# One weight transfer issued as 119 + 9 partitions at the end of a weight stream

## The chip, the cores and the metric

The kernel runs on one core of one Trainium2 chip. A core has five engines that work beside each other and are tied by semaphores: TensorE (PE, matrix products; its weight loads are shown as PEld), VectorE (DVE), ScalarE (ACT), GpSimd (POOL) and SyncE (SP). Sixteen DMA engines move data between the memory outside the core (DRAM) and the 128 partitions of the core's memory; POOL, SP and ACT issue transfers to them, each through a queue of its own. A transfer signals that it has landed through a semaphore, which the engines raise by one each, sixteen in all. The metric is the time of one execution in microseconds (us), as the device measures it; lower is better.

## The reference

The reference runs a sliding-window attention and feeds its result, 8 batches of 576 positions with 512 channels, to a spectral mixing layer:

```python
X = np.fft.rfft(x, axis=1)                       # x: 8 x 576 x 512, out of the attention
Xr, Xi = (np.real(X[:, :n_modes]), np.imag(X[:, :n_modes]))      # 64 modes
Yr = np.einsum('bmd,mde->bme', Xr, w_r) - np.einsum('bmd,mde->bme', Xi, w_i)
Yi = np.einsum('bmd,mde->bme', Xr, w_i) + np.einsum('bmd,mde->bme', Xi, w_r)
Y[:, :n_modes] = Yr + 1j * Yi
y = np.fft.irfft(Y, n=S, axis=1)
u = x + y
return (u + np.maximum(u @ w_ch, 0.0)).astype(np.float32)
```

Each of the 64 modes has a real and an imaginary weight matrix of 512 x 512 float32. Together `w_r` and `w_i` are 128 MB, and each number of them is used once for each batch. They have to come in from DRAM once.

## The kernel before, in words

The kernel does four things that overlap. It computes the attention (units of four score blocks, lines 252 to 345) and the forward transform of its result into `XQ`, with tables of sines. It streams the mode weights in and multiplies them with the transformed input (`mode_half`, line 176). It computes `x @ w_ch` tile by tile (line 610) while the stream goes on. At last it transforms the mixed modes back, adds, applies the rectifier and stores 36 tiles of 128 x 512 (lines 786 to 926).

The weights come in groups of four modes. `steps` (line 98 on) lists (group, half of the 512 input channels); for each step there is one transfer of `w_r` and one of `w_i`. The last steps are those of groups 12 and 13 (`LAST` and `LAST + 1`), so the last transfer brings the `w_i` half of group 13, modes 52 to 55. A transfer turns float32 in DRAM into bfloat16 on its way. Its tile is 128 partitions x 4 modes x 1024 numbers, 1 MB as it lands and 2 MB as it is read: each partition and mode is one row of 2 KB. The page's sizes are those of the landed data.

The list `wlist` (lines 103 to 114) holds these transfers; each entry has a list `parts` of the pieces that it is issued in. For nearly all entries `parts` has one piece of four modes. One early entry (`ONES`) is spread over three separate entries. For the last entry of all, `parts` has three pieces, `[(p, p + 1), (p + 2,), (p + 3,)]`: two modes (512 KB landed, 1 MB read), one mode, one mode.

`load_weights` (line 142) issues transfers from POOL in the order of `wlist`, as far as a buffer is free: a ring `ringA` of three tiles and, earlier, `ringB` of five and some memory lent by other tiles. A transfer into a ring tile waits until TensorE has done the matmuls that read the tile's old contents. At the end of the stream only `ringA` is in use, so POOL issues a transfer when TensorE has finished the one three before it.

`mode_half` issues one step's matmuls for `w_r` or `w_i`. For the last one (`ending`, line 180) the matmuls are sorted by mode, so that those of modes 52 and 53 wait for the first piece alone, those of 54 for the second and those of 55 for the third. The order of TensorE's instructions is the order in which this code calls them. Just ahead of the last half TensorE is given the left-over `x @ w_ch` jobs and the first output tile's start (`late["first"]`, `tail_xw(0)`). Behind it comes the tail: the halves of the last product are cast on VectorE and ScalarE (`cast_halves`, line 626), turned on TensorE (line 648 on), multiplied by `w_ch` (lines 1006 and 1014), and then each output tile takes part in a chain of matmuls, adds and a store.

Of the kernel before, what the change touches and what calls it, by code (L numbers as in the profile page):

```python
# [16 lines left out]

NRA = 3
NRB = 5
WARM = 8  # L20
NEG = -1.0e30
MAGIC = 12582912.0
# [4 lines left out]
def kernel(  # L27
# [10 lines left out]
    nc = tc.nc  # L38
# [10 lines left out]
    HALF = DM // 2  # L49
    NJ = 2  # L50
# [5 lines left out]
    def pool(name, bufs=1, **kw):  # L56
        opened.append(tc.alloc_tile_pool(name=name, bufs=bufs, **kw))
        return opened[-1]
# [32 lines left out]
    ringA = pool("ringA", bufs=NRA, side="right", reuse_waits="tile")  # L91
    ringB = pool("ringB", bufs=NRB, side="right", reuse_waits="tile")
    EARLY = 10
# [11 lines left out]
    for at, (grp, hb) in enumerate(steps):  # L105
        for ri in range(2):
            p = 4 * grp
            if (at, ri) == ONES:
                parts = [[(p, p + 1)], [(p + 2,)], [(p + 3,)]]
            elif (at, ri) == (len(steps) - 1, 1):  # L110
                parts = [[(p, p + 1), (p + 2,), (p + 3,)]]
            else:
                parts = [[(p, p + 1, p + 2, p + 3)]]
# [20 lines left out]
    held = {"a": [], "b": [], "y": []}  # L134
    room = {"a": NRA, "b": NRB, "y": NLY}
    nload = 0
# [5 lines left out]
    def load_weights(n):  # L142
        nonlocal nload
        while nload < len(wlist):
            at, parts, hb, ri = wlist[nload]
            if 2 * n <= sum(len(ps) for ps in parts):
                return
            if nload in lent:
                w = lent[nload]
            else:  # L150
                open_to = "a" if at >= 2 * EARLY else "aby" if at < EARLY + 2 else "ab"
                h = min(open_to, key=lambda h: held[h][0] if len(held[h]) == room[h] else -1)
                if len(held[h]) == room[h]:
                    if held[h][0] not in spent:
                        return
                    held[h].pop(0)
                held[h].append(nload)
                if h == "y":
                    w = lentY
                else:  # L160
                    w = {"a": ringA, "b": ringB}[h].tile([128, 4, NJ, DM], BF16, name="wi" if ri else "wr", tag="wt")
            src = moe_w_i if ri else moe_w_r
            to = 0
            for ps in parts:
                nc.gpsimd.dma_start(  # L165
                    out=w[:, to:to + len(ps)],
                    in_=src[ps[0]:ps[-1] + 1, HALF * hb:HALF * hb + HALF, :].rearrange("g (p j) e -> p g j e", j=NJ))
                for i, p in enumerate(ps):
                    wtiles[p, hb, ri] = w[:, to + i]
                to += len(ps)  # L170
            nload += 1
            n -= to
# [24 lines left out]
    with tc.manual_schedule():  # L197
# [165 lines left out]
        warm = ps_m.tile([128, DM], FP32, name="warm", tag="misc")  # L363
        for _ in range(WARM):
            nc.tensor.matmul(out=warm, lhsT=idle[:, 0:128], rhs=idle, start=True, stop=True)
# [16 lines left out]
        for nm in ("k", "q", "v"):  # L382
            load(1, nm)
        LEAD = 4
        load_weights(LEAD)
        nc.gpsimd.iota(Kb, pattern=[[64, NBLK]], base=0, channel_multiplier=0,
                       allow_small_or_imprecise_dtypes=True)
# [77 lines left out]
        def early_step(it):  # L465
            nonlocal step
            grp = step
            psm = ps_m.tile([128, DM], FP32, name="psm", tag="misc")
            for ri in range(2):
                mode_half(psm, grp, 0, ri, True, True)  # L470
                load_weights(due(it) - loaded())
            nc.scalar.copy(out=Yacc[grp], in_=psm)
            step += 1
# [4 lines left out]
        for it in range(-3, NU + 3):  # L478
# [23 lines left out]
            g = starts.get(it + 2)  # L502
# [3 lines left out]
            g = starts.get(it + 1)  # L506
            if g is not None and g + 2 < NG:
                load(g + 2, "v")
            if it >= 0:
                for f in trig[0:2]:  # L510
                    f()
                del trig[0:2]
            load_weights(due(it) - loaded())
        do_dft(NG - 1)
        while step < EARLY:
# [255 lines left out]
        ps, pu = {}, {}  # L771
# [292 lines left out]
```

## Time and profile before

| what | us |
|---|---|
| median of three runs | 435.42 |
| lowest and highest of them | 435.29, 435.87 |
| the profiled execution: its own time | 435.06 |
| the profiled execution: its span | 433.3 |
| TensorE busy in it | 333.3 (77%) |
| VectorE, ScalarE, POOL busy | 230.1, 180.0, 101.5 |
| share of DMA in the chain that ended last | 60% |
| mean granted TensorE clock | 0.881 |

The span runs from the first to the last instruction of the program; the execution's time has 1.8 us around it. Names on the left of an arrow are written, names on the right are read: `wi<-in_moe_w_i_dram` is a transfer of `w_i` from DRAM into a ring tile named `wi`. `psm` is the accumulator that `mode_half` writes, `XQ` and `XL` hold the transformed input, and L188 is the line of its matmul. In the chain of work that ended last, each piece is what released the next one; a DMA piece is counted from its issue to its landing, so a transfer that was issued early shows the time that it stood in the queue too. The DMA view of a stretch of time gives the mean busy share of the 16 engines in tenths and the GB/s that they moved, in 40 equal slices.

### The profile page before, as it was taken

To read this page: it belongs to the slowest core of one execution; us is meant where nothing else is said; L and a number is where in the kernel's file an instruction comes from. 1 tells how busy PE (TensorE), PEld (TensorE's weight loads), DVE (VectorE), ACT (ScalarE), POOL (GpSimd) and SP (SyncE) were. 2 spreads that over 40 slices of the span, in tenths; PEclk is the share of its full clock that TensorE was granted. 3 is DMA by queue.
4 is the path that set the end of the run, shared out by engine and by line. 5 is a ranking of instruction groups with operands and counts; after the bars stand their busy time and mean duration, and the time that the engine had idled before them with its cause. 6 is when DMAs were issued, how large, how long until landed. Compare 5 with 4: busy or idle time off the path is not lost.

```text
span 433.3 us, 11049 instructions
## 1 busy us (share of the span) xinstructions
PE 333.3 (77%) x4802; PEld 216.2 (50%) x4802; DVE 230.1 (53%) x472; ACT 180.0 (42%) x322; POOL 101.5 (23%) x150
## 2 busy tenths in 40 slices
PE   6999999998999998974208354666676779779994
PEld 3666767576767676651104122334343445445652
DVE  8588687876676776855104111302131315662894
ACT  5666667575766665520202100122121213334742
POOL 8422223222231231113102100012111112110990
PEclk9999999999999999976558656759888869999998
DMA  8999999999999999999999999999999999994798
GB/s 211 211 211 212 211 212 211 211 211 212 211 212 211 211 212 211 212 213 211 212 259 213 217 212 212 212 212 211 209 212 213 208 211 212 212 212 79 248 357 294
DMA packets 47280, 93.64 MB, mean 216 GB/s; under 512 B 2688, under 2 KB 3136, under 8 KB 47232
## 3 DMA queue, kind: packets, MB, share of 16 engines
q0 software_dynamic: 41008, 81.73, 99.7%
q1 hardware_dynamic: 5328, 9.77, 6.6%
q10 hardware_dynamic: 896, 1.44, 0.9%
q8 instruction: 37, 0.61, 0.5%
q14 instruction: 11, 0.09, 0.1%
HBM read 163.58 MB, written 9.44 MB: 399 GB/s over the span
## 4 chain that ended last, share of the span: by engine, by line
DMA 60%; PE 25%; issue 7%; DVE 3%; ACT 2%; POOL 1%; SPq 0%; DVEq 0%; POOLq 0%
DMA wr<-in_moe_w_r_dram 37%; DMA wi<-in_moe_w_i_dram 16%; DMA rawk<-in_k_dram 7%; PE tr L231 4%; PE psm L188 3%; PE s L278 2%; PE s L290 2%; PE s L270 2%; PE pt L298 2%; PE vb L243 2%; PE o L318 1%; PE psz L786 1%; PE psz L610 1%; DMA out_dram<-ut 1%; PE pst L786 1%
## 5 line engine op out<-in xcount | busy, mean ns | idle before, releaser
L610 PE MATMUL psz<-wch,tr 128*128 128x512 f32 x176 | 63.7, 496 | 11.3 <-DMA wch<-in_moe_w_ch_dram 11.0
L756 DVE CAST xw<-psz 128x512 fp32r<-128x512 f32 x36 | 24.9, 692 | 89.0 <-PE psz L610 89.0
L282 DVE TENSOR_REDUCE mx<-s 128x4 fp32r<-128x512 f32 x72 | 49.6, 689 | 26.7 <-PE s L278 26.4
L584 ACT CAST tr<-ptx 128x512 fp32r<-128x512 bf16 x36 | 21.1, 587 | 101.2 <-PE ptx L603 101.2
L188 PEld LDWEIGHTS <-XQ 128*32 128x32 bf16 x448 | 18.6, 176 | 76.0 <-issue 51.7
L165 POOL DMA_DIRECT2D wi<-in_moe_w_i_dram x32 | 23.4, 732 | 101.4 <-PE psm L188 68.2
L188 PE MATMUL psm<-wi,XQ 128*32 128x512 bf16 x208 | 20.8, 475 | 33.9 <-DMA wi<-in_moe_w_i_dram 33.9
L610 PEld LDWEIGHTS psz<-wch,tr 128*128 128x128 f32 x176 | 37.5, 236 | 18.4 <-issue 11.6
L292 ACT ACTIVATE p<-s 128x512 bf16<-128x512 f32 x72 | 39.7, 603 | 12.8 <-PE s L290 12.8
L165 POOL DMA_DIRECT2D wr<-in_moe_w_r_dram x27 | 20.4, 757 | 98.7 <-PE psm L188 50.6
L188 PE MATMUL psm<-wr,XQ 128*32 128x512 bf16 x184 | 19.3, 501 | 27.4 <-DMA wr<-in_moe_w_r_dram 26.8
L235 ACT COPY kT<-tr 128x576 bf16<-128x576 bf16 x32 | 23.2, 725 | 21.3 <-PE tr L231 21.3
L270 PE MATMUL s<-mask_t,ident_bf 128*128 128x512 bf16 x72 | 28.4, 395 | 0.9 <-ACT p L292 0.8
L278 PE MATMUL s<-kT,qT 64*64 64x128 bf16 (+1 forms) x576 | 29.0, 220 | 0.0
L301 DVE COPY pts<-pt 128x1024 bf16<-128x1024 bf16 (+1 forms) x40 | 25.2, 630 | 5.3 <-PE pt L298 4.0
L235 ACT COPY qT<-tr 128x576 bf16<-128x576 bf16 x32 | 23.3, 729 | 10.3 <-PE tr L231 10.3
L278 PEld LDWEIGHTS <-qT 64*64 64x64 bf16 x576 | 17.7, 106 | 18.0 <-issue 17.5
L290 PE MATMUL s<-mx,ident_r 128*128 128x512 f32 x72 | 26.2, 437 | 0.0
L235 ACT COPY vT<-tr 128x576 bf16<-128x576 bf16 x32 | 23.3, 728 | 4.0 <-PE tr L231 3.8
L298 PE MATMUL pt<-ident_bf,p 128*128 128x128 bf16 x288 | 23.3, 220 | 1.5 <-issue 1.3
L635 DVE TENSOR_TENSOR stg<-psm,Yfour 128x512 bf16<-128x512 f32 x10 | 6.9, 691 | 32.8 <-PE psm L188 32.8
L218 POOL DMA_DIRECT2D rawk<-in_k_dram x15 | 8.1, 541 | 63.8 <-PE tr L231 57.6
(211 smaller groups left out, 611.3 us busy)
## 6 DMA issues: line engine op xcount, KB each, us to landing
wi<-in_moe_w_i_dram POOLq DMA_DIRECT2D x29, 1024.0 KB, 19.1
wr<-in_moe_w_r_dram POOLq DMA_DIRECT2D x27, 1024.0 KB, 18.1
out_dram<-ut SPq DMA_DIRECT2D x28, 256.0 KB, 2.8
rawv<-in_v_dram POOLq DMA_DIRECT2D x16, 288.0 KB, 15.4
rawk<-in_k_dram POOLq DMA_DIRECT2D x15, 288.0 KB, 14.4
rawq<-in_q_dram POOLq DMA_DIRECT2D x15, 288.0 KB, 14.3
x_sb<-in_moe_w_r_dram POOLq DMA_DIRECT2D x2, 1024.0 KB, 15.7
Yfour<-in_moe_w_i_dram POOLq DMA_DIRECT2D x1, 1024.0 KB, 14.5
```

Source lines behind the costliest of these rows:

```text
L165: nc.gpsimd.dma_start(out=w[:, to:to + len(ps)], in_=src[ps[0]:ps[-1] + 1, HALF * hb:HALF * hb + HALF, :].rearrange("g (p j) e -> p g j e" ...
L188: nc.tensor.matmul(out=ps[32 * g:32 * g + 32, 0:e], lhsT=of.rearrange("k s b m -> k (s b) m")[:, (3 * j + 1 - ri) * B:(3 * j + 5 - ri) * B ...
L235: nc.scalar.copy(out=to, in_=pt.rearrange("p j n -> p n j"))
L270: nc.tensor.matmul(out=s, lhsT=ident_bf, rhs=mask_t[:, mk], start=True, stop=True)
L278: nc.tensor.matmul(out=s[ro, t, lo:128], lhsT=lq, rhs=kT[ro, 64 * n - 64 + lo:64 * n + 64], start=False, stop=True, skip_group_check=True)
L282: nc.vector.tensor_reduce(out=mx, in_=s, axis=AX.X, op=ALU.max, negate=True)
L290: nc.tensor.matmul(out=s, lhsT=ident_r, rhs=mx.unsqueeze(2).to_broadcast([128, 4, 128]), start=False, stop=True, skip_group_check=True)
L292: nc.scalar.activation(out=p[:, 4 * c2:4 * c2 + 4, :], in_=s, func=ACT_F.Exp, scale=EX_SCALE)
L298: nc.tensor.transpose(out=pt[:, t, :], in_=st[u]["p"][:, t, :], identity=ident_bf)
L301: nc.vector.tensor_copy(out=ps[:, 0:nt, :], in_=pt[:, 0:nt, :])
L610: nc.tensor.matmul(out=pz, lhsT=tr[:, c, :], rhs=wch[:, c, :], start=(c == 0), stop=(c == NDCH - 1))
L756: nc.vector.tensor_copy(out=XW[i], in_=multiply(tr))
```

## The change

The piece of two modes in the last entry is issued as two transfers instead of one: the first takes partitions 0 to 118, the second partitions 119 to 127, both of the same two modes. The two single-mode pieces behind it, and all other transfers, are issued as before. A loop picks the one or two ranges of partitions: two when an entry has several pieces and the piece has two modes, which holds only for that one piece. POOL issues one transfer more; the order on the other engines stays. The matmuls of modes 52 and 53 depend on both transfers.

```diff
+UNEVEN = 119
...
             for ps in parts:
-                nc.gpsimd.dma_start(
-                    out=w[:, to:to + len(ps)],
-                    in_=src[ps[0]:ps[-1] + 1, HALF * hb:HALF * hb + HALF, :].rearrange("g (p j) e -> p g j e", j=NJ))
+                of = src[ps[0]:ps[-1] + 1, HALF * hb:HALF * hb + HALF, :].rearrange("g (p j) e -> p g j e", j=NJ)
+                for lo, hi in ((0, UNEVEN), (UNEVEN, 128)) if len(parts) > 1 and len(ps) == 2 else ((0, 128),):
+                    nc.gpsimd.dma_start(out=w[lo:hi, to:to + len(ps)], in_=of[lo:hi])
                 for i, p in enumerate(ps):
                     wtiles[p, hb, ri] = w[:, to + i]
                 to += len(ps)
```

The rows in DRAM that the two transfers read are the same as before: a mode's 256 channels are dealt to the partitions in pairs, so partition `p` takes channels `2p` and `2p + 1`, 4 KB in a row in DRAM for each mode.

## The prediction

> **What bounds the kernel now.** I read the page's overview first, then the chain of work that ended last, then the DMA view of the seven microseconds in which the weight stream ends, then the order of instructions there.
>
> ```profile
> span 433.3 us, 11049 instructions
> ...
> DMA  8999999999999999999999999999999999994798
> ...
> q0 software_dynamic: 41008, 81.73, 99.7%
> ...
> q8 instruction: 37, 0.61, 0.5%
> ```
>
> The mean busy share of the 16 DMA engines stays at nine tenths in nearly every slice until 396 us, and the queue of POOL's transfers, q0, makes up all of it. The row q8 is fetched program code: 0.5% of 16 x 433.3 us is 35 us, over 37 fetches 0.94 us each, on the same engines.
>
> ```profile
> 367.45 13.88 DMA wr<-in_moe_w_r_dram
> 381.33 0.04 issue
> 381.37 0.67 PE psm L188 x16
> 382.04 0.24 PE psp L648 x4
> 382.28 0.08 issue
> 382.36 1.26 POOL wi L165 x2
> 383.62 12.62 DMA wi<-in_moe_w_i_dram
> 396.24 0.04 issue
> 396.28 0.50 PE psm L188 x3
> ```
>
> The chain (start, duration, what) is one weight transfer after another; the last lands at 396.24 us, and TensorE starts on it 0.04 us later. From there the chain runs to the end through TensorE, VectorE and the stores. So the end moves one for one with the landing of the last weight bytes, as long as TensorE has nothing else left to do.
>
> ```profile
> DMA  9999999888785566655555566433223320000000
> GB/s 234 211 187 211 187 211 199 164 152 164 140 152 105 105 117 117 117 94 105 105 94 94 105 117 117 82 70 70 47 47 59 59 35 12 0 0 0 0 0 0
> ```
>
> This is 390 to 397 us in 40 slices of 0.175 us. The stream does not stop at once: 211 GB/s until 391.2, about 105 (half of the engines) from 392.2 to 394.4, about 60 (four engines) until 396.0. The same is in the trace's record of the last transfer's semaphore, which each of the 16 engines raises once: 391.28, .35, .66, .72, 392.18, .42, .58, .86 (eight early engines), 394.59, 395.00, .19, .29, 396.06, .12, .18, .24 (eight late ones). The record gives no engine's number. All 16 keep one pace: full transfers land every 4.95 us on each of them. The lateness is old: the spread was 1.6 us for the transfer that landed at 25.5 us and 5.0 us for that of 198.9, and it grew by about 0.95 us on one engine after another, which is a code fetch's length. [...]
>
> ```profile
> 391.00:393.00 2.00, 2.00 (x12) 1.37 (x9) 0.43 (x1) 1.97 (x4) 0.00 (x0) 1.00 0.74 139
> 393.00:395.00 2.00, 2.00 (x29) 1.26 (x28) 0.00 (x0) 0.59 (x1) 0.00 (x0) 1.00 0.51 95
> 395.00:396.30 1.30, 0.68 (x10) 0.37 (x5) 0.00 (x0) 0.00 (x0) 0.00 (x0) 1.00 0.16 30
> ...
> 394.56 1.10 PE L188 MATMUL psm<-wi,XL 128*32 128x256 bf16 x12
> 396.28 0.60 PE L188 MATMUL psm<-wi,XL 128*32 128x256 bf16 x4 [0.62 <-DMA wi<-in_moe_w_i_dram]
> ```
>
> Last columns: DMA share and GB/s. From 391.0 on, 2.00 x 139 + 2.00 x 95 + 1.30 x 30 = 507 KB land; at 211 GB/s that is 2.40 us, so level engines would finish at 393.4 instead of 396.24. TensorE bounds it tighter: it only reaches the last half's matmuls at 394.56, and 16 of them take 0.67 us (the row at 381.37), so they would end at 395.2 at best, not at 396.88: no dealing of the bytes can gain more than 1.65 us.
>
> **The change part by part.** *One more issue on POOL.* The three issues at 382.36 take 0.70, 0.57 and 0.55 us, so a fourth adds 0.55 to 0.70 us before the last one. The last issue would end at about 384.8; the earliest engine comes to that transfer's rows after the one before it, which it finishes at 390.06. Cover is over 5 us on POOL's queue, no other transfer of POOL's follows, and no weight transfer queues behind: cost nothing. If the queue ran dry, it would cost those 0.7 us. SP's and ACT's queues issue nothing between 382 and 398.
>
> *One more wait on TensorE.* The first eight matmuls wait for two semaphores instead of one. The "issue" rows after waits are 0.04 us; it falls at 394.56 at the earliest, before the last landing: nothing, at most 0.04.
>
> *How the bytes are dealt out.* This decides. Two modes are 2 x 128 rows of 2 KB, 16 for each engine. An engine's row costs 4.95 us / 32 = 0.155 us (and 2 KB at 211/16 GB/s = 0.155). All partitions in this trace come in 128s, in 16 equal shares; no row shows 119. If shares must stay equal, 119 = 7 x 17 leaves seven engines with 34 rows each, and nine partitions go to nine engines with 2 rows each. So seven engines gain 18 rows, 18 x 0.155 = 2.79 us, and nine lose 14, 2.17 us (if the nine are the others). If shares may be unequal, at most 8 and 1 partitions meet on one engine, 18 rows instead of 16: +0.31 us; the engine left out is up to 16 rows, 2.48 us, earlier.
>
> [...] No run here shows which holds for 119.
>
> *What it does to the end.* With seven shares, if one of the seven is among the four engines that end at 396.06 to 396.24, the end is there plus 2.79: 398.85 to 399.03, later by 2.61 to 2.79 us. If they touch only the late four of 394.59 to 395.29, it ends at 397.38 to 398.08, later by 1.14 to 1.84. If all seven are early engines, the slowest ends at 392.86 or 392.58 plus 2.79, 395.65 or 395.37, and the late ones at 396.24 - 2.17 = 394.07: earlier by 0.59 or 0.87 us. With sixteen shares: between -0.06 (the engine of 396.24 is the one left out, the next is at 396.18) and +0.31. The unknown so lies between -0.87 and +2.79. I take equal shares, because every transfer of the trace has them, and the seven touching the last four, because seven picked as a run of neighbours (my assumption; a random seven would do worse) miss eight late ones only if the early eight are neighbours too and the run starts on their first or second: 2 of 16 starts, or about one of two if the run always begins at one end of a half. Sum: 0 (POOL) + 0 (TensorE) + 2.7 us. The chain behind it has no cover, so all of it shows: the profiled execution took 435.06 us with its span of 433.3, so 437.76; it lies 0.36 us below the median of 435.42, against which I forecast 438.1.
>
> **The rivals.** *Seven early engines take the extra rows (faster).* The mechanism is a levelling: 34 rows fit into the 3.4 to 5 us by which the early half leads, and the nine light engines get 2.17 us back. For it: the split moves 2.79 us one way and 2.17 us the other, across a gap of 3.4 us between the groups' middles. Against it: it needs the right seven. It decides at the point where no engine ending after 393.45 (396.24 - 2.79) is among the seven. Price -0.59 to -0.87: 434.55 to 434.83. [...]
>
> *Shares over all sixteen (no change).* For it: all 16 engines raise every semaphore here. Against it: no unequal share is seen. -0.06 to +0.31: 435.36 to 435.73.
>
> *Only the less late four are hit.* +1.14 to +1.84: 436.56 to 437.26.
>
> *Something else*, such as slower rows on a crowded engine (a row costs 0.155 us at any time here, also when four engines are left: 8 rows between the increments at 395.02 and 396.24) or an empty queue.
>
> **How the numbers follow.** Seven shares with one of the last four: 0.44, time 438.1, own range 437.9 to 438.4. Less late four: 0.05. Early seven: 0.32. Sixteen shares: 0.13. Something else: 0.06 (0.04 slower, 0.02 faster). The bound of 0.2%, 0.87 us, is about what a measurement of this kernel can tell from no change. The early seven end just at it: half, 0.17, is counted as faster and 0.15 as the same. Faster 0.17 + 0.02 = 0.19; same 0.15 + 0.13 = 0.28; slower 0.44 + 0.05 + 0.04 = 0.53. The range reaches from the early seven to the forecast, with 0.1 to 0.2 us for the scatter of runs (435.29 to 435.87): 434.4 to 438.4.
>
> **What would show it.** In the changed kernel's semaphore record of the 119-partition transfer, seven of the sixteen increments should stand about 2.8 us later, and nine 2.2 us earlier, than the steps before them. If the forecast holds, the tail in GB/s has a stretch of one to seven engines (13 to 92 GB/s) up to about 399 us, and TensorE's wait before its last four matmuls grows from 0.62 to about 3.3 us. If the early seven took it, the tail falls off steeply at 394 to 395.7 and that wait shrinks or goes. With sixteen shares the staircase stays. POOL's group at L165 should have one instruction more of 0.5 to 0.7 us. Wrong would be the forecast if the run of seven avoids the late engines, if shares are unequal, or if TensorE had other work in the gap.

## The result, and the profile after

The changed kernel took 439.86 us (median; 439.5, 440.21, 441.0 and 438.0), the kernel before in the same session 435.55 (435.29 to 435.87): a ratio of 1.0093, with a 95% interval of 1.008 to 1.0105. The change is slower by some 4.3 us. The forecast was 438.1 with a range up to 438.4, so its sign was right and its size was not: about 1.8 us are missing from its sum, as the net of two errors that go opposite ways.

The changed kernel's profiled execution took 439.5 us with a span of 437.7. First its overview (the same rows as before):

```profile
span 437.7 us, 11007 instructions
...
DMA  8999999999999999999999999999999999991798
...
q0 software_dynamic: 41344, 81.73, 98.8%
```

The stream is as full as before until its last slices; the queue q0 moves the same 81.73 MB in 336 packets more. Next its chain of work that ended last (start, duration, what), around the landing:

```profile
382.69 2.07 POOL wi L168 x3
384.76 12.99 DMA wi<-in_moe_w_i_dram
...
397.79 0.72 PE psm L189 x3
...
400.46 1.15 PE psz L1007 x4
401.62 0.85 PE psm L1007 x4
402.47 1.71 PE psp L1015 x4
```

POOL starts the last of its four issues at 384.76 and ends it at 385.33, where 384.8 was worked out; the first engine is through with that piece's predecessor at 388.75, so this costs nothing. The last bytes land at 397.75 instead of 396.24: 1.51 us later, not 2.7. The last three rows are the surprise. In the chain of before the same three groups of matmuls are shorter:

```profile
398.13 0.67 PE psz L1006 x4
398.80 0.48 PE psm L1006 x4
399.28 0.93 PE psp L1014 x4
```

The time from the last landing to the end of the span grew from 37.04 to 39.97 us. So 1.51 + 2.93 = 4.44 us, which is the whole difference between the two profiled executions (439.5 against 435.06), and two thirds of it lie behind the landing, where the prediction has nothing.

The windows view, cut on steps of 3.41 us on which the granted clock changes, shows what happened there. Columns: the stretch, its length, busy time and count of PE, PEld, DVE, ACT and POOL, the granted TensorE clock, the DMA share, GB/s. First the changed kernel, then the one before.

```profile
394.51:397.92 3.41, 1.83 (x16) 0.90 (x15) 0.00 (x0) 0.00 (x0) 0.00 (x0) 1.00 0.17 31
397.92:401.33 3.41, 2.75 (x13) 1.66 (x14) 1.12 (x2) 1.50 (x4) 0.00 (x0) 0.50 0.00 0
401.33:404.74 3.41, 3.41 (x14) 2.22 (x12) 0.42 (x1) 0.84 (x2) 0.00 (x0) 0.50 0.14 38
404.74:408.16 3.42, 3.42 (x21) 1.56 (x20) 3.41 (x6) 3.32 (x7) 2.55 (x3) 1.00 0.51 104
```

```profile
394.91:398.32 3.41, 2.38 (x22) 1.35 (x18) 0.91 (x2) 1.06 (x4) 0.00 (x0) 1.00 0.07 13
398.32:401.74 3.42, 3.42 (x23) 2.11 (x22) 1.80 (x4) 2.24 (x5) 0.27 (x1) 1.00 0.14 38
```

In the stretch in which it waits for the last bytes TensorE was busy for 2.38 of 3.41 us before (0.70) and for 1.83 now (0.54). In the changed kernel the granted clock is 0.50 for the next two stretches, 6.83 us, just as the tail begins; in the one before it stays at 1.00 until 429.05.

TensorE's order of instructions there (start, duration, engine and line, what, count, and in brackets the idle time before with what ended it):

```profile
395.49 0.67 PE L189 MATMUL psm<-wi,XL 128*32 128x256 bf16 x8 [0.54 <-DMA wi<-in_moe_w_i_dram]
396.54 0.60 PE L189 MATMUL psm<-wi,XL 128*32 128x256 bf16 x4 [0.39 <-DMA wi<-in_moe_w_i_dram]
397.79 0.92 PE L189 MATMUL psm<-wi,XL 128*32 128x256 bf16 x4 [0.65 <-DMA wi<-in_moe_w_i_dram]
```

Three waits, 1.6 us together, stand in place of one of 0.62. By the record of the semaphores the pieces of modes 52 and 53, of 54 and of 55 have landed at 395.44, 396.50 and 397.75 us, where it was 393.79, 395.02 and 396.24 before: each comes about 1.5 us later, the first of them too. Last the DMA view of 390 to 401 us in 40 slices of 0.275 us:

```profile
DMA  9999989898978773233222111000000000000000
GB/s 165 179 179 150 143 164 186 164 171 164 179 134 149 142 134 67 45 60 60 52 45 37 30 22 30 15 7 0 0 0 0 0 0 0 0 0 0 0 0 0
```

The busy share holds at 0.7 or more until 394.1; then it falls in a step to 0.2 to 0.3 and about 50 GB/s, four engines of sixteen, and trails off. There is no such step before. The record of the semaphores tells the shares. The sixteen increments of the transfer before the split, and of the 119 partitions:

```
last full transfer  386.76 .91 .97 387.11 .14 .15 388.47 .51 | 389.60 390.26 .34 .39 391.15 .45 .58 .89
119 partitions      387.19 .35 .40 390.63 .65 391.34 .64 392.09 .22 .24 .35 .50 393.79 .98 394.85 395.23
```

Of the early eight, three raise it at 387.19 to 387.40, 0.2 to 0.5 us after the last full transfer: they have no row of it. Five come about 5.3 us after it (388.47 to 393.79 for one), 34 rows of 0.155 us. Two of the late eight have 34 rows as well (389.60 to 394.85). So seven engines got the 119 partitions and nine did not. With sixteen equal shares this execution would have ended at 391.89 + 32 x 0.1547 = 396.84 us (the last engine's end of the last full transfer, and its 32 rows of 2 KB at 4.95 us / 32 each); it ended at 397.75. This end is an estimate. The dealing cost 0.91 us of the 1.51; the other 0.60 is the stream of this execution, which was later before the split.

In the rest of the text "late by" is this difference: the last landing less the equal-share end of the same execution. In the kernel before it is 0.03 us.

### The profile page after: what moved, and what is told of

It is laid out like the page before. It is cut to its first block, busy times and chain, and to the rows that moved or that the text cites. A ratio compares the mean times of both kernels' runs of the same rounds, so it can differ in the third digit from the quotient of the medians.

```text
span 437.7 us, 11007 instructions
## 1 busy us (share of the span) xinstructions
PE 324.7 (74%) x4758; PEld 216.9 (50%) x4802; DVE 229.8 (52%) x472; ACT 180.1 (41%) x322; POOL 102.2 (23%) x151
## 3 DMA queue, kind: packets, MB, share of 16 engines
q0 software_dynamic: 41344, 81.73, 98.8%
## 4 chain that ended last, share of the span: by engine, by line
DMA 52%; PE 34%; issue 6%; ACT 3%; DVE 2%; POOL 1%; DVEq 0%; POOLq 0%
DMA wi<-in_moe_w_i_dram 31%; DMA wr<-in_moe_w_r_dram 21%; PE tr L232 5%; PE s L279 4%; PE s L291 3%; PE pt L299 3%; PE vb L244 3%; PE psm L189 3%; PE o L319 2%; PE s L271 2%; PE psz L787 1%; PE pst L787 1%; PE pst L869 1%; PE px L342 1%; ACT qT L236 1%
## 5 line engine op out<-in xcount | busy, mean ns | idle before, releaser
L611 PE MATMUL psz<-wch,tr 128*128 128x512 f32 x176 | 60.9, 477 | 11.2 <-DMA wch<-in_moe_w_ch_dram 11.0
L611 PEld LDWEIGHTS psz<-wch,tr 128*128 128x128 f32 x176 | 36.3, 229 | 18.0 <-issue 11.6
L331 DVE TENSOR_TENSOR x_sb<-o,r 128x512 bf16<-128x512 f32 x32 | 22.1, 691 | 1.1
```

Of the source, the lines that this page charges most:

```text
L331: nc.vector.tensor_tensor(out=xo.rearrange("p c (h d) -> p c h d", d=64), in0=ov[:, :, :, 0:64], in1=rb, op=ALU.mult)
L611: nc.tensor.matmul(out=pz, lhsT=tr[:, c, :], rhs=wch[:, c, :], start=(c == 0), stop=(c == NDCH - 1))
```

## The experiments

Two questions were open. Where does the landing end up, and why not at +2.7 us? And is the tail's 2.9 us a consequence of TensorE's waits, of the lateness as such, or chance? The theory: the 119 partitions go to seven engines in equal shares, which ones being set by a ring; they make the landing late; TensorE's longer waits let its granted clock fall to one half behind the landing. Rivals: the split costs something in itself; the seven can be moved to early engines, so that the change would be faster; the clock falls for another reason.

Each run was timed beside the kernel before. Times are medians with the lowest and highest; the ratios have 95% intervals.

### The change once more

No edit, a second set of runs.

> The changed kernel once more, to see what of its time repeats. Theory A (unequal dealing plus clock): the sixteen increments of the 119-partition transfer again split into seven that come 34 rows (5.3 us) after those of the transfer before and nine that come within 0.5 us; the granted clock falls to 0.5 for one or two steps of 3.4 us right behind the last weight landing, and the tail from that landing to the end of the span is 39 to 41 us where that happens and 37 us where it does not. Time 438 to 441. Theory B (the tail is longer for another reason, say the stores): the tail is 39 to 41 us at a clock of 1.0 too.

Measured: 440.19 us (437.36 to 441.14) against 435.69, ratio 1.0086 [1.006, 1.0112]. The six single times fall into two groups, 437.36 and 437.43, and 440.1 to 441.14; the four of the first set have one at 438.0 and three from 439.5 to 441.0. The profiled one took 440.1: late by 1.65 us (398.47 against 396.82), clock 0.5 for 6.82 us from 398.77, tail from the landing 39.86 us.

```profile
395.36:398.77 3.41, 1.52 (x15) 1.03 (x16) 0.00 (x0) 0.00 (x0) 0.00 (x0) 1.00 0.11 21
398.77:402.18 3.41, 2.75 (x14) 1.73 (x13) 1.12 (x2) 1.50 (x4) 0.00 (x0) 0.50 0.00 0
```

The same picture with other numbers: TensorE busy for 0.44 of the stretch, then half the clock. The dealing is the same (five early and two late engines took the 34 rows), but the landing is late by 0.7 us more. Between the two groups of times there is no direct look at the clock: no execution of the lower group was profiled, and the mean granted clock of a whole execution (0.880 to 0.897 in the three of the lower group, 0.869 to 0.880 in the seven of the upper) points the expected way but scatters as much in the kernel before (0.866 to 0.899).

### The same split in shares that sixteen divides

```diff
-UNEVEN = 119
+UNEVEN = 112
```

> The same split into two transfers, at partition 112 in place of 119: 112 = 16 x 7 and 16 = 16 x 1, so both can be dealt out in equal shares to all sixteen engines. Theory A (the dealing costs): the increments keep the staircase of the kernel before, ratio to it 0.998 to 1.002. Theory C (one more transfer and one more wait cost by themselves): slower by about 4 us, ratio near 1.009.

Measured: 435.85 us (435.41 to 436.58), ratio 1.0004 [0.9995, 1.0013]. The profile keeps the staircase, the last four matmuls wait 0.65 us, TensorE is busy for 2.35 of 3.41 us (0.69), the clock stays at 1.0; late by 0.04 us. A second transfer, its issue on POOL and TensorE's second semaphore cost nothing that can be measured here. What cost the change its 4.3 us is the number 119.

### The small transfer first

The ranges become 9 and 119 partitions, in this order.

```diff
-for lo, hi in ((0, UNEVEN), (UNEVEN, 128)) ...
+for lo, hi in ((0, 128 - UNEVEN), (128 - UNEVEN, 128)) ...
```

> The two transfers in the other order: partitions 0 to 8 first, then 9 to 127. Theory A with a fixed start of the run of engines: the seven engines with 34 rows are now seven of the nine that had 2 rows, and these hold six of the eight late ones, so the last landing comes 2.6 to 2.8 us later than with equal shares, and the time is 440 to 442 with the slow clock behind it. If the order does not move the seven: as the changed kernel, 438 to 441.

Measured: 441.41 us (440.53 to 441.87), ratio 1.0128 [1.0115, 1.0141]. Late by 2.76 us (399.61 against 396.85): one early and six late engines took the 34 rows. DMA from 390 to 401 us:

```profile
GB/s 149 142 112 105 112 134 119 104 127 119 119 119 89 82 104 97 97 74 97 89 82 60 89 82 82 60 89 75 52 45 60 52 30 15 0 0 0 0 0 0
```

The nine others are done by 393.8; from there to 397.7 some 84 GB/s are left, the rate of six to seven engines at 13.2 GB/s each (211 / 16). This is the forecast's case, with its 2.61 to 2.79 us, but it needed the other order of the two ranges. It fits a ring that the nine partitions turned by nine, so that the run of seven began nine engines further on. TensorE's waits were 1.93, 0.54 and 0.64 us, the clock was 0.5 for 6.83 us and the tail 40.48.

### Turning the ring

If the run of seven follows a ring, a small transfer of k partitions ahead should move its start by k, and one of 16 - k behind the last piece should put it back. These transfers bring two rows of eight numbers for each of their partitions into an unused tile.

```diff
+    scrap = consts.tile([16, 2, 2, 8], BF16, name="scrap")
...
+            def turn(i, n):
+                if len(parts) > 1:
+                    nc.gpsimd.dma_start(out=scrap[0:n, i], in_=moe_w_i[0:2, 0:n, 0:8].rearrange("g p e -> p g e"))
...
+            turn(0, 2)
...
+            turn(1, 14)
```

With 2 and 14, 3 and 13, 10 and 6:

> The changed kernel with a tiny transfer of 2 partitions (2 modes of 8 numbers each) issued ahead of the 119-partition one and another of 14 partitions behind the last weight transfer, both into scrap memory that nothing reads. Theory A1 (each transfer of fewer than 16 shares takes the next engines of a ring, and the early eight are neighbours in it, from the third to the tenth counted from where the run of seven began): the run moves by two engines, all seven with 34 rows are early ones, none of the late ones. The last landing is then 0.5 to 1.2 us earlier than with equal shares; the wait before the last matmuls is short, the clock stays 1.0, and the time is 434.5 to 435.3, ratio to the kernel before 0.997 to 0.999. Theory A2 (the start of the run does not move with earlier transfers): as the changed kernel, 437 to 441.

> The same with 3 partitions ahead and 13 behind. Theory A1: the run moves by three engines, again all seven are early ones, and another early engine is left out: last landing 0.5 to 1.2 us earlier than with equal shares, time 434.5 to 435.3. Theory A2: 437 to 441.

> The same with 10 partitions ahead and 6 behind. Theory A1: the run moves by ten engines, and all seven with 34 rows are late ones: the last landing is 2.6 to 2.8 us later than with equal shares, the clock falls to 0.5 behind it, and the time is 440.5 to 442. Theory A2: as the changed kernel, 437 to 441, with five early and two late engines in the seven.

| start of the seven | early and late engines among them | late by, us | median, us | ratio |
|---|---|---|---|---|
| the change's | 5 and 2 | 0.91, 1.65 | 439.86, 440.19 | 1.0093, 1.0086 |
| 2 on | 5 and 2 | 1.06 | 437.55 (436.64 to 438.45) | 1.0044 [1.0031, 1.0058] |
| 3 on | 4 and 3 | 1.98 | 438.89 (437.3 to 440.94) | 1.0082 [1.0056, 1.0108] |
| 9 on (small first) | 1 and 6 | 2.76 | 441.41 | 1.0128 |
| 10 on | 2 and 5 | 2.77 | 440.77 (438.3 to 441.31) | 1.0112 [1.0094, 1.0131] |

The ring holds in these five cases: with each start, other engines carry the 34 rows, in every case seven, and one order of the engines fits all the rows of the table, if each engine is early or late in all these executions. Counted from where the change's run begins, numbers 0, 1, 2, 7 and 8 are early, two of 3 to 6, and one of 10 to 15; the other eight are late. The hope that came with it fell. The expectation for 2 and 3 on was a case faster than before, with seven early neighbours, and both missed it by 2 to 4 us. With 10 on the time lies in the expected range, but two of the seven were early where none was expected. The reason is the same: in this order the early engines are not eight neighbours, and every run of seven holds a late one, those tried two or more. That settles the prediction's faster rival here: by this order no start of the ring brings it about.

### TensorE kept busy while it waits

Matmuls of 128 x 512 on constants, into an accumulator that nothing reads, stand ahead of those of modes 52, 54 and 55: 3, 2 and 4 in the first version, 3, 1 and 2 in the second. They add work and change no value.

```diff
+IDLE = 3, 0, 2, 4
...
+            for _ in range(IDLE[g] if ending and not j else 0):
+                nc.tensor.matmul(out=late["idle"], lhsT=ident_bf, rhs=trigI[:, 0:DM], start=True, stop=True)
...
+                    late["idle"] = bank("z")
```

> The changed kernel with nine more matmuls of 128 x 512 on constant data (3, 2 and 4 of them, 0.22 us each) ahead of the last half's matmuls for modes 52, 54 and 55, where TensorE waits for weights; their result is not used. Theory A (the lower clock is TensorE's idling): the granted clock stays 1.0 behind the last landing, the tail is 37 us again, and the time falls by 2 to 3 us against the changed kernel, to 436.5 to 438. Theory B (the tail is longer for another reason): 439 to 441, no gain.

> As e4 (the change with unused matmuls in TensorE's waits), with 3, 1 and 2 of them in place of 3, 2 and 4, so that they end before the last bytes land. Theory (e4 still paid 0.4 us for its own unused matmuls, and the change's landing costs 0.9 to 1.8 us): clock 1.0 behind the landing, tail 37.0 to 37.6, last matmuls start 0.04 to 0.1 us after the landing: 436.8 to 438.2. Rival (too few matmuls keep the clock up no longer): clock 0.5 behind the landing in some executions, times spread up to 440 as in the change itself.

Measured: 438.45 us (437.92 to 439.29), ratio 1.0072 [1.0059, 1.0085], and 438.18 (436.57 to 438.65), ratio 1.0043 [1.0027, 1.0059]. The first misses its expectation by 0.45 us, the second meets the upper end of its own. The first one's windows, cut on its own steps of the clock:

```profile
396.05:399.46 3.41, 3.36 (x23) 1.58 (x22) 0.00 (x0) 0.00 (x0) 0.00 (x0) 1.00 0.07 14
399.46:402.87 3.41, 3.00 (x21) 2.01 (x19) 1.54 (x3) 1.87 (x5) 0.00 (x0) 1.00 0.00 0
```

Busy for 0.98 instead of 0.54, and the clock stays at 1.0. The landing is no earlier than in the change, it is even later (late by 2.46 and 2.60 us in the two profiles), and still the kernel is faster by 1.4 to 2 us: the tail is 37.18 and 37.10 us instead of 39.97 and 39.86. The group of times from 439.5 to 441.1 is gone. In the first version the unused matmuls ended late, and the last real ones began 0.41 us after the landing; in the second, 0.04.

Two profiles of the turned ring show the same without any added work, and speak against the rival that the split itself lengthens the tail. With 2 and 3 on, the dealing is uneven too and the landing late by 1.06 and 1.98 us, but TensorE is busy for 0.69 and 0.58 of the step at the landing, the clock stays at 1.0, and the tail is 37.25 and 37.46 us. The step of the second:

```profile
396.83:400.25 3.42, 1.97 (x21) 1.02 (x15) 0.43 (x1) 0.46 (x2) 0.00 (x0) 1.00 0.06 11
```

The same with the small transfer first, and 8, 2 and 2 unused matmuls ahead of modes 52, 54 and 55 (the expectation names 53 where it is 52):

```diff
+IDLE = 8, 0, 2, 2
```

> As e3 (9 partitions, then 119), with 8, 2 and 2 unused matmuls of 128 x 512 ahead of those of the last transfer's modes 53, 54 and 55, so that TensorE is busy while it waits; they add work of TensorE and change no value. Theory (of e3's 5.7 us some 2.75 are the late landing and the rest is the granted clock of 0.5 behind it): the landing stays about 2.7 us late, at 398.5 to 399.7, the clock stays at 1.0 behind it, the tail is 37.0 to 37.8 us instead of 40.5: 438.2 to 439.2, against 441.4 of e3. Rival (the clock has other causes than the waits, such as the later landing itself): clock 0.5 for 6.8 us behind the landing, 441 to 442.

Measured: 440.34 us (439.98 to 440.83), ratio 1.0103 [1.009, 1.0116]. The clock stayed at 1.0 (a stretch of 3.41 busy out of 3.41 from 395.64, by the windows view), but only 1.1 us of the median came back, and 438.2 to 439.2 was expected: a miss by over 1 us. The profile (439.98, the fastest of the four) shows a part of why: it lands at 399.61, as the one without unused matmuls does, but these held the last real ones up until 400.40, 0.79 us after the landing. So 1.9 us came back between the two profiles, and why the medians show less is not known. From the start of the last real matmuls to the end it took 37.80 us, against 40.44 without the unused ones: 2.6 us less at the full clock, of which the experiment's own matmuls ate a part.

And the control, the kernel before with four unused matmuls ahead of those of mode 55:

> The kernel before with four unused matmuls of 128 x 512 ahead of the matmuls of mode 55, where TensorE waits 0.6 us for the last landing. Theory A: the clock was 1.0 there already, so nothing is to be gained: ratio 0.999 to 1.002 (the four take 0.87 us where 0.62 us are free, at worst 0.3 us late). If the lower clock also struck executions of the kernel before: faster by 0.2% or more.

Measured: 436.4 us (435.75 to 436.74), ratio 1.0019 [1.001, 1.0027]. The clock is 1.0 with and without them; the last real matmuls began at 397.17, 0.85 us after the landing at 396.32, where 0.3 us at worst was expected. Keeping TensorE busy gained nothing here, where the clock did not fall, and cost its own overrun.

### Late in equal shares

The kernel before, its last transfer whole, with one more transfer ahead of the last pieces: 192 rows of 2 KB into an unused piece of DRAM, 12 rows for each of the sixteen engines.

```diff
+    scrap = nc.dram_tensor("scrap", (96, 2, 2, 512), BF16, kind="Internal").ap()
...
+            if len(parts) > 1:
+                nc.gpsimd.dma_start(out=scrap, in_=src[0:2, 0:192, :].rearrange("g (p j) e -> p g j e", j=NJ))
```

> The kernel before, with the last transfer left whole, and one transfer more issued just ahead of its pieces: 192 rows of 2 KB of the same weights into an unused piece of DRAM, in 16 equal shares of 12 rows, so by the price of a row (0.155 us) 1.86 us for each of the 16 engines. It makes the last bytes late without any uneven dealing, by about what the change's landing was late (0.9 to 2.6 us). Theory (the change costs its late landing, and behind that, from TensorE's longer waits, the granted clock of 0.5 and a tail of 39.5 to 40.5 us): last landing 398 to 398.8, in some executions clock 0.5 for 3.4 or 6.8 us behind it, 437.3 where it stays at 1.0 and 439 to 440.2 where it falls, median 438 to 440. Rival (the drop of the clock belongs to the split: to the seven loaded engines or the three waits on one semaphore more): clock 1.0 in all, tail 37.0 to 37.7, 437.0 to 437.8 with a narrow spread. Rival (rows to DRAM cost other than rows to the core's memory): the landing moves by 1 us or less, or by 3 us or more.

Measured: 437.33 us, ratio 1.005 [1.0032, 1.0068]; the seven times are 437.14 to 437.79 six times, and 440.15. The landing is late by 1.90 us (398.21 against 396.31), as the price of a row has it. The profiled one is of the six:

```profile
395.78 0.67 PE L191 MATMUL psm<-wi,XL 128*32 128x256 bf16 x8 [1.05 <-DMA wi<-in_moe_w_i_dram]
397.00 0.60 PE L191 MATMUL psm<-wi,XL 128*32 128x256 bf16 x4 [0.55 <-DMA wi<-in_moe_w_i_dram]
398.25 0.60 PE L191 MATMUL psm<-wi,XL 128*32 128x256 bf16 x4 [0.66 <-DMA wi<-in_moe_w_i_dram]
```

```profile
393.48:396.90 3.42, 1.91 (x27) 1.17 (x20) 0.00 (x0) 0.48 (x1) 0.00 (x0) 1.00 0.57 107
396.90:400.31 3.41, 2.25 (x16) 1.30 (x16) 0.93 (x2) 1.09 (x4) 0.00 (x0) 1.00 0.07 13
400.31:403.72 3.41, 3.41 (x23) 2.10 (x22) 1.79 (x4) 2.23 (x5) 0.28 (x1) 1.00 0.14 38
```

Lateness alone cost about its own length: late by 1.9 us, +1.6 of the median, tail 37.16. The clock did not fall here although the three waits sum to 2.26 us, more than in the change. The steps of the clock lie otherwise to the waits: two stretches share them, with 0.56 and 0.66 busy. Had a step begun at 394.74, the same instructions would fill only 0.37 of it. The expected median (438 to 440) is missed; that the spread is not narrow, with one time 2.8 us above the median, fits the clock, but that execution was not profiled, so the point stays open: that half the clock also comes without an uneven split is likely and not shown.

### A dealing that levels the engines

Worked out from the order found by turning the ring: in equal shares 51, 4, 38 and 35 partitions would go to 3, 4, 2 and 7 engines in one turn, 34 rows for numbers 0 to 2, 2 for 3 to 6, 38 for 7 and 8, and 10 for 9 to 15.

```diff
-for lo, hi in ((0, UNEVEN), (UNEVEN, 128)) ...
+for lo, hi in ((0, 51), (51, 55), (55, 93), (93, 128)) ...
```

> The last 1 MB transfer goes as four: 51, 4, 38 and 35 partitions. By equal shares these go to 3, 4, 2 and 7 engines, sixteen in all, so one turn of the ring: counted from where the run of seven began, engines 0 to 2 get 34 rows, 3 to 6 get 2, 7 and 8 get 38, 9 to 15 get 10 (16 each before). Theory (shares equal, one ring, engines 0 to 2 and 7 and 8 among the early): all late engines give up at least 6 rows, 0.93 us; the early five go up by 18 or 22 rows, 2.79 or 3.40 us, from 391.3 to 392.9 in the trace of before, so to 394.1 to 396.3. The last landing comes 0 to 0.9 us earlier than with one transfer, TensorE's wait before its last matmuls is shorter and its clock stays at 1.0 behind the landing: 434.5 to 435.5 with the kernel before at 435.4. Rival (the places of early and late engines differ from execution to execution, so no fixed dealing can be right): one of the five is late, landing 2.8 to 3.4 us later, 438 to 441. Rival (three more small transfers cost something in themselves, at POOL or at the engines): 436 to 437 with the last landing early in the engines' record.

Measured: 435.58 us (434.69 to 436.36) against 435.81 (435.28 to 436.84), ratio 0.9991 [0.9982, 0.9999]. The profiled execution ends 0.45 us ahead of its equal-share end (396.32 against 396.77), with TensorE busy for 2.36 of 3.41 us and the clock at 1.0.

```profile
DMA  9999999999789777644330000000000000000880
```

From 390 to 401 us, the tail of the stream is steeper than before. Dealt so, the rows did level the stream, as the prediction's faster rival has it, but that brought 0.2 us of the median, less than the 0.2% (0.87 us) that a measurement of this kernel can tell from no change. A part went to the price of more transfers: a late engine that finished the last full transfer at 391.46 raises the semaphores of the three transfers in which, by this dealing, it has no row at 391.65, 391.83 and 392.00, so 0.17 to 0.19 us for each, and some 0.54 us of the 0.93 that six rows less give would be spent on that.

## Why the prediction was wrong, point by point

- **What bounds the kernel.** Right: the stream until its end, then the chain behind it. The end moved with the landing one for one where the clock stayed (landing +1.97 us and time +2.08 between the profiles of the kernel before and the one late in equal shares).
- **POOL's issue and TensorE's second semaphore at nothing.** Right within what can be measured: 435.85 against 435.69 with 112 and 16. POOL's four issues took 2.64 us instead of 1.81, so 0.83 more where 0.55 to 0.70 was worked out, under the same cover.
- **Equal shares, seven engines with 34 rows and nine with 2.** Right, and the prices too: a run of seven fits all eight kernels that issue 119 partitions, at about 5.3 us for 34 rows.
- **"One of the seven among the last four", +2.61 to 2.79 us.** Wrong in both profiles of the change: the term of 2.7 us measured 1.51, of which the dealing is 0.91, and the second profile was late by 1.65. The same dealing with unused matmuls was late by 2.46 and 2.60 us, near the forecast. The forecast took one profile's staircase as fixed. Going back 50 rows of 0.1547 us from the last landing, the nearest increments of the last full transfer, within 0.3 us, are those at 390.26 and 390.78 in the change and 391.24 and 391.43 in the other two. By this estimate the engine that set the end was among the first four of the late eight in both profiles of the change, and among the last four in the others. So the change's profiles are the rival "only the less late four", whose +1.14 to +1.84 us holds the 1.51, and which had a chance of 0.05. Why the order among the late engines changes from one execution to the next was not tested.
- **The seven and the early eight as neighbours.** The seven fit as neighbours on a ring for all five starts tried; in that order the early eight are not neighbours. The rival of seven early engines had 0.32 on that assumption, and has nothing for any start of the ring.
- **TensorE's wait before its last four matmuls grows to 3.3 us.** Wrong in form: every piece landed late, by 1.65, 1.48 and 1.51 us against the profile of before, and there are three waits, 0.54, 0.39 and 0.65 us.
- **"The chain behind it has no cover, so all of it shows: 437.76."** This is the step that failed most. It takes the tail as a constant, 37.04 us. It is 39.97 in the profile, 2.93 more, because the granted clock is 0.5 for 6.83 us from 397.92. Where unused matmuls hold the clock, the tail is 37.1 to 37.2 and the medians are 438.45 and 438.18, beside the 438.1 of the forecast (with the landing late by 2.46 and 2.60 us, as forecast, in their profiles, and 0.41 us of overrun in the first); the change itself has 439.86. The sum lacks a term of 2.8 to 2.9 us that seems to apply in most executions: of ten times of the change three are from 437.36 to 438.0 and seven from 439.5 to 441.14, and both profiled ones of the upper group show the half clock behind the landing.

What the sum should have been for the profiled execution: 435.06 + 0.60 (this execution's stream) + 0.91 (dealing) + 2.93 (clock) = 439.5. Against the forecast's 437.76 the clock adds 2.93 us and the landing, 1.51 instead of 2.7, takes 1.19 back. That the forecast missed by no more than 1.74 us is luck.

## What to carry to other kernels

Price a split by the engine with the largest share: here 112 and 16 partitions, both of which sixteen divides, cost nothing that showed (ratio 1.0004), and 119 and 9 put 34 rows instead of 16 on seven engines (1.0093). When a change makes TensorE wait longer just ahead of a serial stretch, look at the granted clock of that stretch and at the busy share of the 3.41 us before it; here half the clock behind the waits cost 2.9 us, more than the 1.5 us of the later landing. Unused matmuls in the gap kept the clock up, but where they ended after the data had landed they cost their overrun, 0.4 to 0.9 us. Aiming a dealing at the early DMA engines brought little: even with the whole ring known it gave 0.2 us.

## What the runs showed of the hardware

**In these runs the granted clock went with TensorE's busy share in the 3.413 us before.** In all fourteen profiles the changes of the granted clock lie on a grid of 3.413 us, to within 0.005 us in one execution, and the grid lies otherwise to the program in each. The busy share of TensorE in each step of the grid (the matmuls' spans as the profile models them; the first 20 and last 8 us left out) sorts what comes next:

| clock in the step | busy share of the step | steps | clock of the next step |
|---|---|---|---|
| 1.0 | below 0.46 | 116 | 0.5 in all |
| 1.0 | 0.46 to 0.57 | 80 | 0.5 in 19, 1.0 in 61 |
| 1.0 | above 0.57 | 1076 | 1.0 in all |
| 0.5 | below 0.81 | 245 | 0.5 in all |
| 0.5 | 0.81 to 0.84 | 14 | 1.0 in 6, 0.5 in 8 |
| 0.5 | 0.85 and above | 129 | 1.0 in all |

So in these steps the clock fell only where TensorE had been busy for 0.57 or less, as behind the change's landing (0.54), where no single wait in the step is longer than 0.65 us, and it rose only where that share was 0.81 or more. From 0.46 to 0.57 the same range of shares stood before both clocks, 0.5 in 19 steps and 1.0 in 61. This could explain the two groups of times, the same waits in one step or shared by two as the grid happens to lie, but that was not shown. The kernel before has 0.70 busy in the step at its landing; the profiles of the change have 0.54 and 0.44, those with 9 partitions first or the ring turned by ten 0.36 and 0.26. The runs with unused matmuls are the test by intervention; the table alone is a correlation.

**Three transfers cost one engine 0.17 to 0.19 us each where, by the dealing, it had no share in them**: that is the time from one increment to the next on the one engine of the levelled kernel whose increments stand apart from the others'.

**In the kernel late in equal shares a row to DRAM cost about what a row to the core's memory did**: between the sixteen increments of the last full transfer and those of the 12 rows, each taken in order, lie 1.86 to 1.96 us, 1.92 in the mean, so 0.16 us for each row of 2 KB against 0.155.
